# One core, linear attention followed by a gated long convolution: PSUM as four tiles of two banks, gates, forward outputs and inverse products in pairs, the identity matrix made on VectorE, and a new order of the instructions

## The chip, the core and the metric

The kernel runs on one core of one Trainium2 chip. The metric is the device time of one execution in microseconds (us). TensorE (PE) multiplies matrices into PSUM, VectorE (DVE) and ScalarE (ACT) read PSUM and compute elementwise, GpSimd (POOL) makes index patterns and issues the loads, and SyncE (SP) issues the stores and the moves inside the chip's memory.

## The reference, cut to what matters

Eight batches of eight heads, 576 rows of 64 features. An attention with positive random features is followed by a projection to three streams, a circular convolution of the second stream along the rows (in the frequency domain), a product of the three and an output projection.

```python
q_p, k_p = phi(q * scale), phi(k * scale)        # exp(x @ omega.T - |x|^2/2 - max) / sqrt(128)
kv = einsum('bhsm,bhsd->bhmd', k_p, v);  z = sum(k_p, axis=2)
attn = einsum('bhsm,bhmd->bhsd', q_p, kv) / (einsum('bhsm,bhm->bhs', q_p, z)[..., None] + 1e-6)
x = attn.transpose(0, 2, 1, 3).reshape(8, 576, 512)
x1, x2, x3 = split(x @ w_proj, 3)
y = x1 * irfft(rfft(x2, axis=1) * rfft(filter_fft, axis=0), n=576, axis=1) * x3
out = y @ w_out                                   # (8, 576, 512) float32
```

## The kernel before, in words

The 576 rows of a batch are four tiles of 128 rows and a rest of 64; the rests of two batches share one tile ("left", "rest"). The batches are worked in four pairs.

The attention of a batch has these stages, named in the code by `nc.at(...)`. "keys" turns the loaded keys (`transposes`, L634, eight 128x128 transposes into one PSUM tile, copied to `kt` or `klt` by VectorE), multiplies them with omega and takes the exponential on ScalarE into `ek` (`key_features`, L678). "values" finds the largest feature of each row (`max_to_c`, tiles `h1` and `mx`) and scales the values with its reciprocal (`vc`, `vcl`). "queries" gives `eqt` in the same way. "sums" multiplies `ek` with `vc` into `kv`. "turn out" multiplies `eqt` with `kv`, divides (`normalise`, L698: `rden`, then `xb`) and turns the result into `xt` (`turn_runs`, `turn_back`). For batches 5 to 7 the turns of keys, queries and output are DMA transposes issued by SP (`cross`).

The second half has the stages "fold" and "rest" (sums of thirds of the rows, `xf`, times the middle third of `wproj` into `x2`), "gates" (L1054: for each of four column blocks a product `p1` and a product `p3`, each four matmuls of 512 columns; ScalarE copies `p1` to `x1`, VectorE multiplies `p3` with it into `x13`), "forward" (L1152: four products with the tables `fwb`, `fwa`, copied by ScalarE one by one to `sp` and `xs`; SP swaps the halves of `sp` into `sw`), a product with the filter's spectrum (`hps`, `hqs`, made once from the loaded filter and moved by SP), "inverse" (L1215: for each of two column blocks a pair of products in `pa` and then two products `pb`, each added to `ya` by VectorE, two subtractions and two products into `yt` and `ytl`) and "out" (products with `wout`, scaled by ScalarE, stored by SP).

PSUM has eight banks of 512 fp32 values. Before, they are held by three rings (L269 to L276): two tiles of two banks ("a2": features, queries, sums, turn out), three of one bank ("h": everything of the second half) and one of one bank ("t": transposes).

Nothing of this is issued as it is called. A `Plan` records each operation (consecutive matmuls into one tile form one operation) and works out which one depends on which; then `issue` sends them out in the order of the constant `ORDER`, a list of all 1,349 operation numbers written out by hand. An operation of the list goes to the end of its engine's queue, and each engine takes its queue strictly in order; so the list sets the order on PE, ACT, DVE, POOL and SP, the order of the loads among them, and which tile of a ring is taken when. All matmul, copy and load lines of the profile carry the line of that call, L228, so groups are told apart by their tiles.

At the start, `first_constants` (L323) makes the index patterns `fi` and `si` with iota on POOL and the 128x128 identity with the library's `make_identity`, also on POOL; every transpose needs the identity. `make_residues` and `sines` (from L403 and L472) work out the sine tables from `si`, on ACT (`yt`, then the sines) and DVE in turns.

```python
def two_banks():
    return nc.tile(psum, [P, 2, 512], FP32, name="a2", bufs=2)
def bank():
    return nc.tile(psum, [P, 512], FP32, name="h", bufs=3)
def bank_t():
    return nc.tile(psum, [P, 512], FP32, name="t", bufs=1)
...
for op in self.order():
    for real, name, args, kw in op.calls:
        ...
        getattr(real, name)(*args, **kw)
```

Of the kernel before, what the change touches and what calls it, by code (L numbers as in the profile page):

```python
# [12 lines left out]
FP32 = mybir.dt.float32  # L13
# [8 lines left out]
P = 128  # L22
# [4 lines left out]
31 32 28 30 4 3 29 35 26 37 38 55 0 1 2 39 22 5 44 40 45 41 42 139 48 7 46 141 36 11 49 27 70 47 10  # L27
50 43 69 33 51 52 8 34 6 71 57 23 25 53 54 140 72 73 58 24 74 84 85 137 75 586 587 15 60 62 63 86 59
87 64 56 211 585 61 96 66 88 68 590 97 21 65 89 90 91 12 210 67 9 148 106 108 92 17 149 151 153 150
152 154 100 593 101 102 155 107 103 94 109 157 159 98 156 158 588 104 99 105 142 110 112 164 111 113  # L30
13 160 161 114 162 165 136 163 146 20 19 82 79 76 16 145 115 122 123 124 119 222 223 125 126 180 120
127 181 121 116 117 234 235 170 118 14 166 167 93 591 168 95 169 172 628 134 135 175 171 177 128 129
225 173 595 216 629 623 227 130 131 18 592 594 597 624 178 179 174 228 589 229 236 77 81 630 176 194
237 144 132 143 133 195 196 644 599 596 632 224 219 214 226 248 600 188 615 631 189 190 249 617 191
185 80 147 607 192 193 609 230 232 186 187 605 238 598 201 202 78 606 218 182 220 633 231 239 240
197 198 601 183 203 204 603 602 294 625 295 184 616 205 604 618 645 199 206 200 669 207 646 656 657
650 666 608 611 233 613 246 722 612 247 610 241 208 347 724 256 209 257 659 346 250 258 288 259 667
660 670 671 672 636 665 627 260 296 298 251 252 673 282 674 658 661 262 723 614 289 138 253 254 291
668 243 290 649 648 662 293 292 647 687 675 634 358 725 255 688 297 299 261 626 359 242 244 689 637
638 641 635 640 690 264 370 639 642 676 681 304 682 305 263 265 371 663 707 709 710 364 221 306 664  # L40
708 269 277 212 217 480 213 683 307 684 308 685 309 686 654 643 651 655 278 270 279 365 215 701 702
711 266 320 321 677 703 271 267 268 678 652 322 704 360 653 272 691 695 245 692 680 696 679 698 323
324 731 318 273 706 362 302 303 319 730 732 619 712 699 694 697 700 621 274 275 693 733 300 341 718
749 342 343 276 620 301 750 751 720 372 310 312 752 373 622 753 754 738 743 755 714 280 740 739 315
311 756 713 757 719 744 281 317 313 351 83 741 721 705 726 734 374 742 745 746 747 758 810 314 367
728 811 736 316 483 352 344 345 369 735 785 786 787 325 812 326 715 284 285 286 283 349 473 829 830
327 788 817 789 737 748 790 818 328 329 330 828 375 727 813 814 729 376 716 377 717 759 361 366 782
368 363 386 387 388 389 287 479 783 836 336 382 333 334 335 424 837 383 760 815 816 885 844 761 762
350 348 418 845 331 332 887 791 337 765 338 792 793 339 340 763 764 766 820 832 431 430 881 432 433
883 357 384 886 882 378 380 833 767 819 884 427 426 834 822 385 429 428 821 390 888 784 768 770 391  # L50
769 852 835 823 853 485 392 831 434 435 397 399 826 356 450 827 394 771 396 773 379 772 850 776 851
451 400 354 401 436 437 438 398 824 777 838 439 825 839 393 395 452 774 775 864 865 778 779 840 841
454 846 475 847 453 848 410 411 913 872 915 866 867 873 405 780 412 381 353 854 406 407 781 448 449
843 842 849 855 800 468 469 889 413 801 870 871 802 470 471 869 414 858 856 862 794 472 797 415 795
484 355 798 891 416 868 488 491 417 861 914 857 859 425 490 860 879 916 893 922 895 402 863 493 476
806 796 799 420 917 807 919 918 874 403 404 408 809 441 445 409 447 443 878 880 808 923 894 920 896
921 477 421 419 875 1008 906 905 907 890 897 924 925 927 908 899 892 926 877 876 440 444 446 803 804
442 928 898 900 989 929 930 933 492 487 931 489 932 934 992 455 456 457 1007 939 993 994 901 940 461
462 463 941 494 1015 903 942 464 478 990 458 995 482 474 943 1072 1016 1074 1073 902 465 805 459 466
1031 460 1075 904 935 422 486 936 938 909 495 937 496 467 1029 911 1030 1032 1064 1066 950 513 497  # L60
955 952 951 956 953 944 945 1065 1067 498 515 514 518 516 499 500 501 1009 502 954 536 957 503 910
958 507 946 960 1084 520 538 539 1086 540 964 965 541 1085 912 1023 1087 562 1011 991 542 543 563
545 970 971 1024 1060 1062 544 1061 1076 1078 999 508 1012 1010 959 998 505 1063 481 1000 967 1013
1014 947 948 509 510 511 968 517 519 564 1005 1001 996 969 972 1002 966 982 423 512 546 565 1006 997
566 983 521 1025 1045 1003 522 523 1033 1046 949 547 548 549 526 527 528 550 551 524 1017 537 1026
979 1027 1028 525 1004 980 1018 1019 984 532 533 1034 1020 961 962 985 986 534 529 1035 530 1077
1069 1043 531 1022 1021 1044 504 506 560 1040 1041 1079 1042 1037 963 981 988 535 1038 973 556 1036
561 974 1068 1070 580 1080 558 1039 1107 553 581 1071 1082 582 1187 1108 1110 1111 1109 555 1092
1096 1094 1099 552 987 1047 975 1048 1058 557 1168 1101 1098 1097 1100 1102 1103 1057 559 1051 583
1112 1113 1104 1093 554 1095 573 574 1106 1081 570 1173 1083 1052 1049 1050 1174 1088 1090 584 1105  # L70
575 1089 571 567 1114 1115 1116 1140 1141 572 1053 1059 1091 976 576 577 1054 1247 1142 1143 977
1144 1249 1145 568 1055 1186 1056 1188 578 1243 1245 1171 1172 1118 1119 1120 1248 569 1121 1123
1250 1117 1122 1124 1244 1125 579 1246 1126 1169 1128 1190 1191 1149 1150 1129 1194 1131 1195 1178
1170 1189 1259 1130 1261 1239 1241 1132 1134 1196 1135 1133 1177 1136 1137 1139 1179 1210 1192 1211
1197 1193 1175 1176 1202 1203 1260 1204 1151 1208 1262 1205 1184 1138 1182 1209 1185 1198 1199 1127
1152 1183 1153 978 1201 1200 1206 1207 1240 1161 1242 1220 1219 1212 1213 1221 1214 1180 1271 1181
1162 1163 1230 1273 1154 1164 1231 1165 1166 1167 1272 1216 1274 1217 1218 1228 1229 1224 1225 1222
1223 1232 1155 1156 1227 1215 1157 1226 1275 1276 1277 1263 1265 1233 1235 1278 1280 1264 1279 1281
1266 1234 1282 1158 1159 1251 1253 1286 1283 1284 1252 1288 1287 1254 1291 1292 1289 1255 1146 1290
# [57 lines left out]
class Plan:  # L137
# [14 lines left out]

    def at(self, stage, b):
        self.where = stage, b

    def _new(self, eng, name):
        op = Op(eng, len(self.ops), name, self.where)
        self.ops.append(op)
# [1196 lines left out]
```

## Time and profile before

| what | value |
|---|---|
| three runs | 261.46, 261.57 and 497.8 us; median 261.57 us |
| the profiled execution | 261.35 us, of which the span from its first to its last instruction is 259.6 us |
| granted TensorE clock | 0.999 |
| PE busy / ACT busy / DVE busy / POOL busy in the span | 238.8 / 195.6 / 210.6 / 63.4 us |
| PE busy from 0 to 32.5 us, from 32.5 to 227.5, from 227.5 to 259.6 | 18.7 of 32.5, 192.1 of 195.0, 28.0 of 32.1 us |
| exponentials and copies of 128x1024 from PSUM on ACT | 1.03 to 1.04 us each |
| copies of 128x512 from PSUM on ACT | 0.59 to 0.60 us each |
| bytes moved | 35.26 MB, mean 136 GB/s |

The profile is of one execution. A row of a timeline reads: start in us from the span's start, duration in us, engine, line, operation, out<-in by the program's names, shape, and in brackets the engine's idle time before it and what ended it. Operations of one engine overlap somewhat: of two in a row the second starts before the first has ended. In the page's slices each digit is the busy share of a fortieth of the span in tenths.

### The profile page before, as it was taken

The page shows a single profiled execution, that of the slowest core. Times are in us where ns is not written, and L with a number is a line of the kernel's source. Part 1 is how long each engine was busy: PE and PEld are TensorE (multiplying, and loading weights), DVE is VectorE, ACT ScalarE, POOL GpSimd, SP SyncE. Part 2 cuts the span into 40 slices and gives each one's busy share as a digit, 9 for nine tenths or more (in the row PEclk, how much of TensorE's full clock was granted, in tenths as well). Part 3 has the DMA queues.
Part 4 walks back from the last instruction along what each step waited for, and adds up shares of the span by engine and source line. Part 5 has one row for each costly group of instructions (what it writes and reads, how often), then busy time and mean ns, then how long its engine had stood idle before and what let it go on. Part 6 is the DMA issues. An engine that isn't in the chain of part 4 may idle for free.

```text
span 259.6 us, 5722 instructions
## 1 busy us (share of the span) xinstructions
PE 238.8 (92%) x2218; PEld 136.5 (53%) x2250; DVE 210.6 (81%) x474; ACT 195.6 (75%) x309; POOL 63.4 (24%) x88
## 2 busy tenths in 40 slices
PE   0488789999999999999999999999999999999994
PEld 0355555655656656555663554546556554465441
DVE  4889998399998899797899685998989974398880
ACT  3999399899898969999697939977584655575543
POOL 8374843870018610533039000000000000000000
PEclk9999999999999999999999999999999999999999
DMA  5999999999239999699979955027660160053226
GB/s 66 165 147 189 193 200 202 176 185 173 44 94 153 170 201 147 91 209 172 169 182 158 186 102 107 3 76 166 188 162 0 43 167 37 24 161 121 108 80 217
DMA packets 86786, 35.26 MB, mean 136 GB/s; under 512 B 58219, under 2 KB 81256, under 8 KB 86760
## 3 DMA queue, kind: packets, MB, share of 16 engines
q0 software_dynamic: 59616, 17.31, 64.1%
q1 hardware_dynamic: 27000, 17.47, 27.4%
q8 instruction: 17, 0.28, 0.4%
q10 hardware_dynamic: 144, 0.13, 0.1%
q14 instruction: 9, 0.07, 0.1%
HBM read 34.64 MB, written 9.44 MB: 170 GB/s over the span
## 4 chain that ended last, share of the span: by engine, by line
PE 82%; DVE 10%; ACT 4%; issue 2%; POOL 1%; DVEq 0%; POOLq 0%; ACTq 0%
PE h L228 64%; PE a L228 13%; PE t L228 5%; DVE h L228 2%; ACT L228 1%; DVE bt L228 1%; DVE xb L228 1%; DVE vc L228 1%; ACT yt L228 1%; DVE kt L228 1%; DVE qt L228 1%; ACT gtab L228 1%; DVE mx L228 0%; DVE x L228 0%; ACT xt L228 0%
## 5 line engine op out<-in xcount | busy, mean ns | idle before, releaser
L228 PE MATMUL h<-xt,wproj 128*128 128x512 bf16 x244 | 62.6, 379 | 0.6
L228 ACT CAST x<-h 128x512 bf16<-128x512 f32 x68 | 39.7, 596 | 12.4 <-PE h L228 11.4
L228 PEld LDWEIGHTS <-wproj 128*128 128x128 bf16 x384 | 31.3, 98 | 25.8 <-issue 1.7
L228 ACT ACTIVATE osb<-h 128x512 f32<-128x512 f32 (+4 forms) x49 | 27.6, 567 | 16.4 <-PE h L228 9.5
L228 ACT ACTIVATE eqt<-a 128x1024 bf16<-128x1024 f32 x32 | 32.6, 1042 | 1.3 <-PE a L228 1.3
L228 ACT ACTIVATE ek<-a 128x1024 bf16<-128x1024 f32 x32 | 32.3, 1031 | 1.0 <-PE a L228 0.7
L228 PE MATMUL h<-wproj,xf 128*128 128x512 bf16 x124 | 31.9, 380 | 0.2
L228 PE MATMUL h<-wout,yt 128*128 128x512 bf16 x122 | 31.3, 379 | 0.6 <-DVE yt L228 0.2
L228 DVE TENSOR_TENSOR x<-h,x 128x512 bf16<-128x512 f32 x32 | 21.8, 686 | 11.6 <-PE h L228 10.9
L228 POOL DMA_DIRECT2D qn<-in_q_dram x26 | 23.2, 901 | 26.6 <-DMA qt<-qn 15.4
L228 DVE TENSOR_TENSOR bt<-h,osb 128x384 f16<-128x384 f32 x32 | 16.9, 551 | 9.6 <-PE h L228 5.4
L228 PEld LDWEIGHTS <-xf 128*128 128x128 bf16 x134 | 12.5, 100 | 13.4 <-issue 1.0
L228 PE MATMUL h<-x,fwb 128*128 128x512 bf16 x65 | 18.6, 379 | 0.4 <-issue 0.2
L228 PEld LDWEIGHTS <-yt 128*128 128x128 bf16 x128 | 11.6, 98 | 13.5 <-DVE yt L228 0.7
L228 DVE TENSOR_TENSOR xb<-a,rden 128x512 bf16<-128x512 f32 x24 | 16.3, 688 | 0.5
L228 PE MATMUL h<-gtab,xs 128*128 128x384 bf16 x64 | 15.7, 327 | 0.1
L228 ACT CAST xs<-h 128x512 bf16<-128x512 f32 x16 | 9.4, 595 | 8.3 <-PE h L228 8.1
L228 PEld LDWEIGHTS <-eqt 128*128 128x128 bf16 x256 | 11.5, 98 | 6.1 <-DVE xb L228 1.2
L228 PE MATMUL a<-om,kt 64*128 64x128 bf16 x256 | 11.9, 226 | 2.2 <-DVE kt L228 1.5
L228 PE MATMUL a<-kv,eqt 128*128 128x65 bf16 x256 | 12.8, 194 | 1.0 <-DVE xb L228 0.7
L228 PE MATMUL t<-ident,kn 128*128 128x128 bf16 x80 | 6.9, 237 | 7.2 <-POOL ident masks.py:199 6.9
L228 PEld LDWEIGHTS <-kt 64*128 64x128 bf16 x256 | 8.2, 97 | 7.9 <-issue 4.2
(157 smaller groups left out, 479.8 us busy)
## 6 DMA issues: line engine op xcount, KB each, us to landing
out_dram<-osb SPq DMA_DIRECT2D x24, 256.0 KB, 2.3
vn<-in_v_dram POOLq DMA_DIRECT2D x8, 512.0 KB, 7.3
kn<-in_k_dram POOLq DMA_DIRECT2D x7, 512.0 KB, 9.7
qn<-in_q_dram POOLq DMA_DIRECT2D x24, 128.0 KB, 8.0
sw<-sp SPq DMA_DIRECT2D x16, 128.0 KB, 2.4
wproj<-in_moe_w_proj_dram POOLq DMA_DIRECT2D x3, 512.0 KB, 12.1
qn<-in_q_dram POOLq DMA_DIRECT2D x2, 512.0 KB, 8.8
out_dram<-xf SPq DMA_DIRECT2D x4, 256.0 KB, 2.0
```

Of the source, the lines that this page charges most:

```text
L228: getattr(real, name)(*args, **kw)
```

## The change

All of PSUM becomes one ring of four tiles of two banks (name "a2"). `bank` and `bank_t` take such a tile and use its first bank alone. The two products of a gate block (`p1`, `p3`), the outputs 2 and 3 and the outputs 0 and 1 of a forward transform, the rest's two products and the two products `pb` of an inverse block share a tile, one bank each; the new `split` keeps their matmuls separate operations in the plan. The forward outputs are now copied two at a time (one ScalarE copy of 128x1024 in place of two of 128x512), and the two additions of an inverse block are one (128x768 in place of two of 128x384). Gates keep their copy and their product.

The identity is no longer made by `make_identity` on POOL, but by one VectorE comparison of the pattern `si` with a new iota `fp` (the partition's number).

The list `ORDER` is new throughout: it has 1,318 operations, and the order on every engine differs. In the head, POOL issues both halves of the first keys ahead of the iotas, the first two parts of `wproj` (the gates') ahead of the values of batch 1, and the filter later; PE has the transposes of both key halves, omega and the left keys first, gates of batch 0 stand ahead of the sums of batch 1, and all four turns of batch 0's output come before them too. On ACT the dummy sine comes first, so that two table loads are issued in place of three. On SP the transposing DMA of the keys of batch 5 stands ahead of the first swaps and of the filter's moves.

```diff
--- before.py
+++ after.py
@@ -24,63 +24,62 @@
 ORDER = """
-31 32 28 30 4 3 29 35 26 37 38 55 0 1 2 39 22 5 44 40 45 41 42 139 48 7 46 141 36 11 49 27 70 47 10
...
+29 30 31 33 34 32 35 139 0 56 27 28 57 8 1 3 4 38 140 39 2 40 6 23 5 41 42 43 45 46 47 50 49 44 51
...
 """
@@ -143,6 +142,7 @@
         self.nc, self.tc = nc, tc
         self.ops = []
         self.where = "start", 0
+        self.fresh = False
         self.tensor = Proxy(self, "PE", nc.tensor)
         self.vector = Proxy(self, "DVE", nc.vector)
         self.scalar = Proxy(self, "ACT", nc.scalar)
@@ -152,6 +152,9 @@
 
     def at(self, stage, b):
         self.where = stage, b
+
+    def split(self):
+        self.fresh = True
 
     def _new(self, eng, name):
         op = Op(eng, len(self.ops), name, self.where)
@@ -177,6 +180,7 @@
         last = self.ops[-1] if self.ops else None
         join = (
             eng == "PE"
+            and not self.fresh
             and last is not None
             and last.eng == "PE"
             and last.where == self.where
@@ -184,6 +188,8 @@
                 last.writes[0][0] == outs[0].tensor.name
             )
         )
+        if eng == "PE":
+            self.fresh = False
         if join:
             op = last
         else:
@@ -267,13 +273,13 @@
     psum = ctx.enter_context(tc.tile_pool(name="psum", bufs=4, space=bass.MemoryType.PSUM))
 
     def two_banks():
-        return nc.tile(psum, [P, 2, 512], FP32, name="a2", bufs=2)
+        return nc.tile(psum, [P, 2, 512], FP32, name="a2", bufs=4)
 
     def bank():
-        return nc.tile(psum, [P, 512], FP32, name="h", bufs=3)
+        return nc.tile(psum, [P, 2, 512], FP32, name="a2", bufs=4)[:, 0]
 
     def bank_t():
-        return nc.tile(psum, [P, 512], FP32, name="t", bufs=1)
+        return nc.tile(psum, [P, 2, 512], FP32, name="a2", bufs=4)[:, 0]
 
 
     nat_tiles = {}
@@ -318,6 +324,7 @@
     nc.sync.dma_start(out=om_f[:], in_=omega[:, :])
     ident = nc.tile(const, [P, P], BF16, name="ident")
     fi = nc.tile(const, [P, 4], FP32, name="fi")
+    fp = nc.tile(const, [P, 1], FP32, name="fp")
     si = nc.tile(hy, [P, 1024], FP32, name="x2", bufs=2)
 
     def first_constants():
@@ -327,7 +334,10 @@
         for r in (slice(0, 64), slice(64, 128)):
             iota(fi[r, 1:3], pattern=[[-385, 2]], base=385, channel_multiplier=3)
         iota(si[:, 0 : 2 * CH], pattern=[[1, 2 * CH]], base=0, channel_multiplier=0)
-        nc.opaque("POOL", lambda: make_identity(tc.nc, ident[:]), ident[:], 650.0)
+        iota(fp[:], pattern=[[0, 1]], base=0, channel_multiplier=1)
+        nc.vector.tensor_scalar(
+            out=ident[:], in0=si[:, 0:P], scalar1=fp[:, 0:1], scalar2=None, op0=ALU.is_equal
+        )
         nc.where = was
 
     load_main(0, "k", 2, first_constants)
@@ -1056,20 +1066,22 @@
             x13 = nc.tile(hy, [P, CB, SM], BF16, name="x13", bufs=3)
             x13s.append(x13)
             for nb in range(CB):
-                p1, p3 = bank(), bank()
+                two = two_banks()
+                p1, p3 = two[:, 0], two[:, 1]
                 for pp, off in ((p1, 0), (p3, 2 * DM)):
+                    nc.split()
                     for ct in range(CB):
                         nc.tensor.matmul(
-                            out=pp[:],
+                            out=pp,
                             lhsT=wproj[:, ct, off + nb * P : off + (nb + 1) * P],
                             rhs=xt_tiles[b][:, ct, 0:SM],
                             start=(ct == 0),
                             stop=(ct == CB - 1),
                         )
                 x1 = nc.tile(hy, [P, DM], BF16, name="x1", bufs=2)
-                nc.scalar.copy(out=x1[:], in_=p1[:])
+                nc.scalar.copy(out=x1[:], in_=p1)
                 nc.vector.tensor_tensor(
-                    out=x13[:, nb, :], in0=p3[:], in1=x1[:], op=ALU.mult
+                    out=x13[:, nb, :], in0=p3, in1=x1[:], op=ALU.mult
                 )
 
         def spectrum(xs, sp, sw):
@@ -1156,28 +1168,29 @@
                 sp = nc.tile(hy, [P, 2, DM], BF16, name="sp", bufs=2)
                 xss.append(xs)
                 sps.append(sp)
-                for m in (2, 3, 0, 1):
-                    pf = bank()
-                    if m < 3:
-                        for kt_ in (2, 0, 1):
+                for pair in ((2, 3), (0, 1)):
+                    two = two_banks()
+                    for m in pair:
+                        pf = two[:, m % 2]
+                        nc.split()
+                        if m < 3:
+                            for kt_ in (2, 0, 1):
+                                nc.tensor.matmul(
+                                    out=pf,
+                                    lhsT=fwb[:, 3 * m + kt_, :],
+                                    rhs=x2[:, kt_, :],
+                                    start=(kt_ == 2),
+                                    stop=(kt_ == 1),
+                                )
+                        else:
                             nc.tensor.matmul(
-                                out=pf[:],
-                                lhsT=fwb[:, 3 * m + kt_, :],
-                                rhs=x2[:, kt_, :],
-                                start=(kt_ == 2),
-                                stop=(kt_ == 1),
+                                out=pf, lhsT=fwar[:, bb, :], rhs=x2l[:], start=True, stop=False
                             )
-                    else:
-                        nc.tensor.matmul(
-                            out=pf[:], lhsT=fwar[:, bb, :], rhs=x2l[:], start=True, stop=False
-                        )
-                        nc.tensor.matmul(
-                            out=pf[:], lhsT=fwa[:], rhs=x2[:, 3, :], start=False, stop=True
-                        )
-                    nc.scalar.copy(
-                        out=xs[:, m, :] if m < 2 else sp[:, m - 2, :], in_=pf[:]
-                    )
-                    if m == 3:
+                            nc.tensor.matmul(
+                                out=pf, lhsT=fwa[:], rhs=x2[:, 3, :], start=False, stop=True
+                            )
+                    nc.scalar.copy(out=(xs if pair[0] == 0 else sp)[:], in_=two[:])
+                    if pair[0] == 2:
                         sw = nc.tile(hy, [P, 2, DM], BF16, name="sw", bufs=2)
                         nc.sync.dma_start(out=sw[lo64], in_=sp[hi64])
                         nc.sync.dma_start(out=sw[hi64], in_=sp[lo64])
@@ -1193,8 +1206,10 @@
             gates(2 * i + 1)
             nc.at("rest", 2 * i + 1)
             x13l = nc.tile(hy, [P, CB, 2, SL], BF16, name="x13l", bufs=1)
-            p1, p3 = bank(), bank()
+            two = two_banks()
+            p1, p3 = two[:, 0], two[:, 1]
             for pp, off in ((p1, 0), (p3, 2 * DM)):
+                nc.split()
                 for nb in range(CB):
                     for ct in range(CB):
                         nc.tensor.matmul(
@@ -1205,9 +1220,9 @@
                             stop=(ct == CB - 1),
                         )
             x1 = nc.tile(hy, [P, DM], BF16, name="x1", bufs=2)
-            nc.scalar.copy(out=x1[:], in_=p1[:])
+            nc.scalar.copy(out=x1[:], in_=p1)
             nc.vector.tensor_tensor(
-                out=x13l[:].rearrange("p n b s -> p (n b s)"), in0=p3[:], in1=x1[:], op=ALU.mult
+                out=x13l[:].rearrange("p n b s -> p (n b s)"), in0=p3, in1=x1[:], op=ALU.mult
             )
 
             ytl = nc.tile(hy, [P, CB, 2, SL], BF16, name="ytl", bufs=1)
@@ -1234,23 +1249,24 @@
                     nc.scalar.copy(out=ya[:, 0], in_=pav)
                     nc.scalar.mul(out=ya[:, 1], in_=pav, mul=3.0)
                     y = nc.tile(hy, [P, 2, 3, CH], FP16, name="bt", bufs=2)
+                    two = two_banks()
                     for u in range(2):
                         ns = slice((2 * g + u) * P, (2 * g + u + 1) * P)
-                        pb = bank()
+                        nc.split()
                         for m in range(3):
                             nc.tensor.matmul(
-                                out=pb[:, 0 : 2 * CH],
+                                out=two[:, u, 0 : 2 * CH],
                                 lhsT=sp[:, 0, ns] if m == 2 else xs[:, m, ns],
                                 rhs=gtab[:, m, :],
                                 start=(m == 0),
                                 stop=(m == 2),
                             )
-                        nc.vector.tensor_tensor(
-                            out=y[:, u, 0:2],
-                            in0=pb[:, 0 : 2 * CH].rearrange("p (j r) -> p j r", j=2),
-                            in1=ya[:, 0, u].unsqueeze(1).to_broadcast([P, 2, CH]),
-                            op=ALU.add,
-                        )
+                    nc.vector.tensor_tensor(
+                        out=y[:, :, 0:2],
+                        in0=two[:, :, 0 : 2 * CH].rearrange("p u (j r) -> p u j r", j=2),
+                        in1=ya[:, 0].unsqueeze(2).to_broadcast([P, 2, 2, CH]),
+                        op=ALU.add,
+                    )
                     nc.vector.tensor_tensor(
                         out=y[:, :, 2], in0=y[:, :, 0], in1=y[:, :, 1], op=ALU.add
                     )
```

## The prediction

> **What bounds the kernel now.** I read the page first, for the sums over the span and its slices.
>
> ```profile
> span 259.6 us, 5722 instructions
> ...
> PE 238.8 (92%) x2218; PEld 136.5 (53%) x2250; DVE 210.6 (81%) x474; ACT 195.6 (75%) x309; POOL 63.4 (24%) x88
> ...
> PE   0488789999999999999999999999999999999994
> ...
> DVE  4889998399998899797899685998989974398880
> ACT  3999399899898969999697939977584655575543
> ...
> DMA  5999999999239999699979955027660160053226
> ```
>
> TensorE is full from the sixth or seventh slice to the last; only the head and the very end have room. Busy time does not say how full, since matmuls overlap, so I count columns. Groups of four 512-column matmuls start 0.86 us apart (236.18 and 237.04 in the timeline): 0.215 us each, 0.42 ns a column. The program issues 556,672 columns: 233.8 us of PE work. The last matmul ends at 255.8 us, so 22.0 us are lost in all. The timeline of PE says where.
>
> ```profile
> 6.94 1.01 PE L228 MATMUL t<-ident,kn 128*128 128x128 bf16 x8 [6.94 <-POOL ident masks.py:199]
> ...
> 10.82 0.59 PE L228 MATMUL t<-ident,kl 128*128 128x128 bf16 x4 [2.62 <-DVE om L228]
> ...
> 30.03 0.43 PE L228 MATMUL a<-kv,eqt 128*128 128x65 bf16 x8 [0.49 <-DVE xb L228]
> ...
> 31.80 0.61 PE L228 MATMUL t<-ident,xb 128*128 128x128 bf16 x4 [0.79 <-DVE xb L228]
> ...
> 36.75 0.19 PE L228 MATMUL a<-vcl,ekl 128*128 128x65 bf16 x1
> 36.78 0.29 PE L228 MATMUL a<-vc,ek 128*128 128x65 bf16 x4
> ...
> 41.13 1.02 PE L228 MATMUL h<-xt,wproj 128*128 128x512 bf16 x4
> ```
>
> The rows at 36.8 end the key sums of batch 1 ("sums 1"). In the program's order 16.4 us of PE work stand up to there, and they end at 37.0: 20.6 of the 22.0 us are lost by then, and 1.4 us in the 219 us after. The first dense filler (gates, h<-xt,wproj) starts at 41.1. So the change can win only in the first 37 us, and can lose anywhere after.
>
> What paces the head is the third reading, the timelines of ACT and DVE.
>
> ```profile
> 12.79 1.02 ACT L228 ACTIVATE ek<-a 128x1024 bf16<-128x1024 f32 x1
> ...
> 26.41 0.59 ACT L228 CAST kv<-a 128x520 bf16<-128x520 f32 x1 [0.59 <-PE a L228]
> 29.58 0.58 ACT L228 COPY qlt<-t 128x512 bf16<-128x512 bf16 x1 [2.57 <-PE t L228]
> 31.11 1.02 ACT L228 ACTIVATE eqt<-a 128x1024 bf16<-128x1024 f32 x1 [0.95 <-PE a L228]
> ```
>
> ACT starts its exponentials at 12.8, after three table loads, does 13 of them in a row, then idles 3.5 us before 31.1 while DVE works off rden, xb and kt. The chain of waits runs through DVE from 17.8 to 35.6. Loads land in the order of issue: by the trace's semaphores v of batch 0 at 20.9, v of batch 1 at 31.4, wproj at 37.5, 41.0 and 46.1. From 16.1 to 33.5 us 2.9 MB (as written) landed: 0.165 MB/us.
>
> **What the Trainium skill says.** "ScalarE: Activation LUTs", What ACT_TABLE_LOAD costs: about 1283 ns; the trace agrees (1283 ns, three). "Perfetto Trace Analysis", Optimizing Scalar/DVE Operations: a fixed cost per operation, about 51 ns for ScalarE and 125 ns for VectorE on PSUM, so pairing is worth little; the trace agrees in size (below). The same page, Optimization Strategy: a gap that repeats on the engine that should be full can mean too few buffers; no such gap shows in this trace after 37 us. "PSUM — Partial Sum Buffer", The four PSUM rules: a matmul's output is at most one bank, so every single-bank user of the new two-bank tiles leaves a bank empty; the six tiles of before become four.
>
> **The change part by part.**
>
> *Pairs.* Forward outputs: 16 ACT copies of 1024 in place of 32 of 512. Two 512 copies in a row take 1.07 and one 0.60, so one more costs 0.48; two exponentials of 1024 take 1.95 and one 1.03, so 0.92. Gain 16 x 0.04 = 0.6 us of ACT. Inverse: 16 adds of 768 for 32 of 384; 384 takes 0.551 and 512 0.687, 1.06 ns a column, so 768 about 0.96 against 1.02 for two: 1.0 us of DVE. Both are hidden under PE (ACT 75% and DVE 81% busy); if the cover failed in the tail they would be worth under 0.1 us there. Gates keep their copies and products: nothing.
>
> *Identity.* It needs si (iota on POOL), now behind both halves of the first key load (0.92 + 0.76 us from 0.84) and the other iotas (0.32, 0.15, a new one, 0.47): ready about 3.75, in place of 2.86. ACT's first yt then starts at 3.8 (before 4.27, because the first table load waited) and ends at 4.45. In DVE's order the identity stands behind nine residue operations that wait for the yt; before, they took from 5.00 to 9.22. After: 4.5 + 3.7 = 8.2 us for the identity, against 6.9. All of PE waits behind it, and on DVE two small residue fixes, the copy kt and om. So the start is lost by 1.3 us (bounds 0 and 2).
>
> *The first exponential.* With four tiles, the transposes of both key halves, omega and the left keys run in a row: 8.2 + 1.0 + 0.3 + 0.5 + 0.9 = 10.9 (before, one t tile: the second half only at 12.17). om is there at 10.6. Key features 11.0, exponential at 11.55 against 12.79. ACT is free by then: one table load fewer (1.28 us), since the first one now serves Sin and the yt. Gain 1.2 us.
>
> *Head, walked to sums 1.* ACT: 13 exponentials at 0.92 to 0.97 with one gap of 0.6 for batch 1's first kt copy. v of batch 0 lands at 21.4 (k of batch 2 now goes ahead of it, but two left loads don't), plus 1.2 for vc: sums 0 at 22.7, kv at 24.1 (26.4 before). q of batch 1 lands at 24.4; turning out batch 0 needs four rden and xb (0.2 + 0.6 each in a row) from 25.7 to 28.9, then four turns, and ACT's four xt copies end at 32.0, where before the last one, put behind sums 1, ended at 40.35. The moved loads: wproj's two gate parts go ahead of v of batch 1; from 15.1 us (1.625 MB) at 0.165 to 0.17, they land at 27.9 and 31.0, and v of batch 1 at 34.0 (31.4 before). vc ends at 35.6. In the meantime PE has filler that it lacked: four gate groups, 16 x 0.215 = 3.4 us, from 32.5. Sums 1 starts at 36.7 (tile free after batch 0's gate product) and ends at 38.0. By then the new order has issued 21.6 us of PE work. Lost: 38.0 - 21.6 = 16.4, against 20.6. **Gain 4.2 us.** Bounds: 6 (loads quicker), 1 (below).
>
> *After the head.* SP: the cross transpose of keys 5 now stands ahead of the swaps xw and sw and the filter's hps and hqs; it waits for k of batch 5 (about 59 us by bytes) and takes 6.6, and the first user of what is queued behind it comes after 65 us of PE work, 82 us: hidden. w_proj's third part lands at 41 and is wanted at 42 to 43. PSUM: from 40 to 100 us of PE work, a tile's banks are taken again a median of 1.71 us after their last write (2.56 before); from 160 on 2.13 (1.49 before). The readers need 1.03 (exponential) or 0.2 + 0.69 (rden, xb). Summing ACT's and DVE's queues up to each reader against the PE work issued meanwhile, I find no group after sums 1 that comes short by more than a few tenths in either order. Nearest row of before: 1.4 us lost after 37. I add 0.4 (bounds -0.5 and +18, below).
>
> *Tail.* Before, PE waits 0.17 us for yt at 252.19 and in gaps of about 0.1. The new order keeps five groups (4.3 us) between the last inverse product and the last output, and DVE's chain there is 3.5 us plus gate product and yt, 1.4: about even, -0.2.
>
> Sum: -4.2 + 0.4 - 0.2 = -4.0 on the profiled execution's 261.35 (span 259.6): 257.3; it stands 0.2 under the median 261.57, so 257.5.
>
> **The rivals.**
>
> *Loads set the head* (0.20). For: DMA reads 9 from the second slice on, and v of batch 1 is later by 2.6 us. Against: it has no gap now either. At 0.15 MB/us v lands at 36.7, sums 1 ends at 40.5, gain 1.7: 260. The late identity passed on in full ends about there too.
>
> *Loads and ACT quicker than walked* (0.14): v of batch 1 at 32.2, sums 1 at 36.2: gain 6, 255.5.
>
> *Slower: four tiles are too few* (0.16). Place: 40 to 160 us of PE work, 167 tiles. With 1.71 us to reuse, an exponential (1.03 + 0.05) leaves 0.63: one 512 copy ahead of it on ACT fits (0.48), two (0.96) come 0.33 late. A third of the tiles so: 56 x 0.33 = 18.5 us, 276. It decides (past 266.8, beyond 2%) from 28 tiles. Against: the queue sums above.
>
> **How the numbers follow.** The forecast (256 to 259.2) has 0.50, so 257.5. About 2%, 5.2 us, is what a measurement of this kernel can tell from no change. Faster: 0.14 and a third of the forecast's 0.50, 0.30. Slower: 0.14 of the third rival. The rest is 0.56. Range 254.5 to 265.5: it leaves out the third rival's far end and little below.
>
> **What would show it.** Right: PE starts near 8.2 behind DVE's ident; the first exponential near 11.5; two table loads; gates before sums 1; sums 1 ends near 38; PE dense afterwards. Wrong: PE waits for ACT or DVE of a few tenths repeated after 45 us (third rival), vc waiting for the v load past 36 (first), or a last matmul not 3.5 to 4.5 us earlier than 255.8.

## The result and the profile after

| | before | after |
|---|---|---|
| median (executions) | 261.6 us (261.5 to 263.1) | 274.0 us (271.0 to 274.6) |
| profiled execution (its span) | 261.35 (259.6) us | 271.0 (269.2) us |
| PE's last matmul ends at | 255.8 us | 264.7 us |
| mean granted clock of the profiled execution | 0.999 | 0.990 |

The changed kernel is slower: the ratio of the mean times is 1.043, 95% interval 1.034 to 1.052, where 0.984 was forecast. Measured again beside the experiments, it is 273.7 us against 261.6, ratio 1.043 (1.039 to 1.048). Single executions in a slow state, such as the one of 497.8 us before, are left out of every median and ratio.

The page of the kernel after, its busy times and slices (PEclk is the granted TensorE clock, in tenths of full speed):

```profile
span 269.2 us, 5682 instructions
...
PE 239.6 (89%) x2218; PEld 139.3 (52%) x2250; DVE 210.2 (78%) x459; ACT 193.8 (72%) x292; POOL 62.6 (23%) x87
...
PE   0687969999978898999999999989997999999993
...
PEclk9997999999999999999999999999999999999998
```

PE is as busy as before (239.6 and 238.8 us), over 9.6 us more span. Before, its slices were full from the seventh on; now there are sevens and eights between the twelfth slice and the thirty-first. The forecast's own marks in the head come true: in the timeline of PE the transposes start behind VectorE's identity at 8.87 (8.2 was forecast), and gates stand ahead of the sums of batch 1. But one row should not be there:

```profile
8.87 1.01 PE L234 MATMUL a<-ident,kn 128*128 128x128 bf16 x8 [8.87 <-DVE ident L234]
...
32.98 1.02 PE L234 MATMUL a<-xt,wproj 128*128 128x512 bf16 x3
36.23 1.02 PE L234 MATMUL a<-xt,wproj 128*128 128x512 bf16 x4 [2.23 <-ACT x L234]
...
40.80 0.29 PE L234 MATMUL a<-vc,ek 128*128 128x65 bf16 x4
```

The row at 32.98 is p1 of a gate block (the record of one of its four matmuls is missing), the one at 36.23 its p3. Between them PE stands 2.2 us until ACT's copy of p1, `x` in the trace, has ended. p3 doesn't use that copy. The same pair in the middle, PE's rows first and then those of ACT's timeline:

```profile
74.33 1.03 PE L234 MATMUL a<-xt,wproj 128*128 128x512 bf16 x4
77.00 1.02 PE L234 MATMUL a<-xt,wproj 128*128 128x512 bf16 x4 [1.64 <-ACT x L234]
```

```profile
74.53 1.01 ACT L234 CAST sp<-a 128x1024 bf16<-128x1024 f32 x1
75.44 1.02 ACT L234 COPY qt<-a 128x1024 bf16<-128x1024 bf16 x1
76.34 0.61 ACT L234 CAST x<-a 128x512 bf16<-128x512 f32 x1
```

p1 is done at 75.4, but ACT has `sp` and `qt` to do first, starts the copy of p1 at 76.34 and ends it at 76.95; p3 starts 0.05 us later. PE's waits, the longest in total first:

```profile
PE a L234 <- ACT x L234: 10.0, 11, 2.2
PE a L234 <- DVE ident L234: 8.9, 1, 8.9
PE a L234 <- ACT eqt L234: 1.3, 3, 0.5
PE a L234 <- DVE qt L234: 1.1, 1, 1.1
```

Eleven waits for ACT x, 10.0 us, of 0.3 to 2.2 us each, all in front of gate products (one of them a rest's). The group of the gates' matmuls, before and after, with its idle time at the end of the line:

```profile
L228 PE MATMUL h<-xt,wproj 128*128 128x512 bf16 x244 | 62.6, 379 | 0.6
L234 PE MATMUL a<-xt,wproj 128*128 128x512 bf16 x245 | 62.0, 379 | 10.6 <-ACT x L234 9.7
```

The program that is built from the kernel agrees: the first matmul of p3 waits for a semaphore of ScalarE in 21 of the 22 blocks whose copy of p1 stands ahead of p3 in the list.

### The profile page after: what moved, and what is told of

The parts are those of the page before. It is cut to its first block, busy times and chain, and to the rows that moved or that the text cites. A ratio compares the mean times of both kernels' runs of the same rounds, so it can differ in the third digit from the quotient of the medians.

```text
span 269.2 us, 5682 instructions
## 1 busy us (share of the span) xinstructions
PE 239.6 (89%) x2218; PEld 139.3 (52%) x2250; DVE 210.2 (78%) x459; ACT 193.8 (72%) x292; POOL 62.6 (23%) x87
## 4 chain that ended last, share of the span: by engine, by line
PE 73%; ACT 14%; DVE 5%; DMA 3%; issue 3%; POOL 0%; ACTq 0%; DVEq 0%
PE a L234 73%; ACT x L234 4%; DMA vn<-in_v_dram 3%; ACT ek L234 2%; ACT eqt L234 2%; ACT xt L234 1%; ACT osb L234 1%; DVE xt L234 1%; DVE x L234 1%; ACT qt L234 1%; ACT eql L234 1%; DVE vc L234 0%; ACT xtl L234 0%; DVE yt L234 0%; ACT xs L234 0%
## 5 line engine op out<-in xcount | busy, mean ns | idle before, releaser
L234 PE MATMUL a<-xt,wproj 128*128 128x512 bf16 x245 | 62.0, 379 | 10.6 <-ACT x L234 9.7
L234 ACT CAST x<-a 128x512 bf16<-128x512 f32 x68 | 39.8, 594 | 33.5 <-PE a L234 33.2
L234 DVE TENSOR_TENSOR x<-a,x 128x512 bf16<-128x512 f32 x32 | 22.0, 690 | 21.8 <-PE a L234 12.0
L234 ACT ACTIVATE osb<-a 128x512 f32<-128x512 f32 (+4 forms) x49 | 27.6, 571 | 13.0 <-PE a L234 10.4
L234 POOL DMA_DIRECT2D qn<-in_q_dram x26 | 23.3, 901 | 38.8 <-PE a L234 15.3
L234 PE MATMUL a<-wproj,xf 128*128 128x512 bf16 x121 | 31.6, 380 | 0.7 <-DVE xb L234 0.2
L234 PE MATMUL a<-wout,yt 128*128 128x512 bf16 x122 | 30.9, 379 | 0.3
L234 DVE TENSOR_TENSOR bt<-a,osb 128x768 f16<-128x768 f32 x16 | 15.2, 952 | 5.7 <-ACT osb L234 5.6
L234 PEld LDWEIGHTS <-xf 128*128 128x128 bf16 x134 | 12.1, 99 | 12.8 <-DVE xf L234 0.5
L234 PE MATMUL a<-x,fwb 128*128 128x512 bf16 x70 | 18.3, 380 | 0.2
L234 PE MATMUL a<-gtab,xs 128*128 128x384 bf16 x64 | 15.6, 326 | 0.0
L234 PE MATMUL a<-om,kt 64*128 64x128 bf16 x256 | 12.3, 229 | 0.7 <-ACT eqt L234 0.5
L234 POOL DMA_DIRECT2D kn<-in_k_dram x9 | 8.0, 889 | 20.7 <-DMA kt<-kn 12.8
L234 PE MATMUL a<-vc,ek 128*128 128x65 bf16 x256 | 11.9, 199 | 0.6 <-DVE vc L234 0.6
```

## The experiments

Theory A: p1 and p3 now share a PSUM tile. They lie in different banks, and the plan (which compares regions) sees no tie between the copy of p1 and p3; but the program that is built from it makes p3, a write into the tile, wait for the copy, a read of the tile. Theory B, the prediction's slow rival: four tiles of two banks are too few. Times are medians; the kernel before had 261.55 us in the first set, 261.6 to 261.75 in the others. A "tie" below is such a wait between instructions that share nothing but a tile.

**The changed kernel again.** 

> The changed kernel unaltered, as the yardstick of this set. Both theories: 271 to 275 us, with about eleven waits of TensorE for ScalarE's copies x, 10 us in all. If the lower granted clock (0.99 where the kernel before had 0.999) comes from the waits, it shows here again; if it was that chip's, it does not.

273.7 us, clock 0.978 to 0.998. The trace names ten waits for ACT x, 7.8 us; the eleventh, 2.2 us ahead of the same first p3 (here at 37.23, when ACT's copy has just ended at 37.17), it puts down to a load, `kl`. So the eleven waits repeat, and so does the lower clock.

**Copies put behind p3, or ahead of it.** In the list, shown for two blocks (620 and 1049 are p1, 621 and 1050 p3, 622 and 1051 the copy):

```diff
-620 228 622 621
+620 228 621 622
```

> The changed kernel with one edit in the order: in the 22 gate blocks where ScalarE's copy of p1 stands ahead of the product p3 in the list, the copy is put directly behind p3. TensorE's own order stays. Theory A (p3 shares its tile with p1, so that p3 is made to wait until the copy of p1 has read the tile, though it lies in the other bank): the 10.0 us of waits for ACT x go, some of them come back as waits for the next reader; 261 to 264 us, TensorE waits for ACT x below 1 us, granted clock 0.99 or more. Theory B (four tiles are too few, a tile is wanted before its reader is done): the waits move to the next tile, 268 us or more.

```diff
-1049 1050 492 494 1051
+1049 1051 1050 492 494
```

> The opposite of the run before: in the 14 gate blocks where the copy of p1 stood behind p3, it is put between p1 and p3, so that all 36 have this order. Theory A: each of the 14 now makes TensorE wait for the copy, at least 0.6 us for the copy and 0.1 for the hand-over, more where ScalarE has other work first: 14 x 0.75 = 10 us or more, 281 us or above. Theory B: the tiles are taken and freed in the same order, 0 to 2 us.

Behind p3: 268.2 us, 5.5 less. Ahead of p3 in all 36: 282.0, 8.3 more, with 20 waits for ACT x, 15.3 us. The second is A's number and excludes B's. The first is B's number (268 or more), not A's. PE's waits in it say why:

```profile
PE a L234 <- DVE x L234: 2.9, 7, 0.7
...
PE a L234 <- DVE x13l L234: 1.6, 2, 1.4
...
PE a L234 <- ACT x L234: 0.7, 1, 0.7
```

Waits for ACT x are down to 0.7 us, but 4.5 us have come for DVE's products of p3 with the copy, the last readers of gate tiles. That is either B, or A turned round: a copy behind p3 has to wait until p3 has been written, 0.86 us, though it reads only p1, and the tile is held that much longer. The changed kernel itself shows this second direction, in a block whose copy stands behind p3. PE's row holds p1 and p3, eight matmuls:

```profile
37.50 1.90 PE L234 MATMUL a<-xt,wproj 128*128 128x512 bf16 x8
```

```profile
39.44 0.59 ACT L234 CAST x<-a 128x512 bf16<-128x512 f32 x1 [0.80 <-PE a L234]
```

p1 is written after half of PE's row, at about 38.5; but ACT stands idle for 0.80 us and starts the copy at 39.44, 0.04 us after p3's end at 39.40.

**Identity early.** In the list with the copies behind p3 (operation 7 is the comparison that makes the identity; it stood further behind):

```diff
-41 42 43
+41 7 42 43
```

> As the run with the copies behind p3, and the identity's comparison moved in VectorE's order from behind the nine residue operations to ahead of the first of them. Theory A on the head: the identity is there at about 4.5 us in place of 8.8, TensorE starts when the first keys land (5.7), the copy kt follows the residues at about 9.2 in place of 9.9, and the first exponential starts at 11.5 in place of 12.1, held by ScalarE's table load: 0.6 us faster than without it. Rival: the head is paced by the loads of v, so nothing is gained (0 +- 0.2).

266.9 us, 1.3 less than without, but the intervals overlap (1.016 to 1.023 against 1.020 to 1.027): no gain is shown, and neither of the two numbers is excluded.

**Fewer large tiles.** Three kernels with the changed kernel's list and early identity. Where the list would start a tile that is not free, the operation moves back.

```diff
-name="a2", bufs=4
+name="a2", bufs=3                       # second and third kernel: bufs=2
-two = two_banks(); p1, p3 = two[:, 0], two[:, 1]
+p1, p3 = gate_bank()[:], gate_bank()[:] # ring "h" of one-bank tiles: 2, or 4
```

> The changed kernel with its list (copies of p1 where it has them, identity early), and the gates' p1 and p3 taken from a ring of two one-bank tiles of their own, so that only three tiles of two banks are left for all the rest; 69 of the 1,318 operations move back where a tile would not be free. Theory A (the shared tile is what costs: p3 waits for the copy of p1, and with the copy put behind p3 the copy waits for p3, so that the tile is held longer): waits for ACT x fall below 2 us though the rest has a tile less; 259 to 264 us. Theory B (four tiles of two banks are too few): with three it is worse than with four, 270 us or more.

> As the run with the gates in tiles of their own, but PSUM as two tiles of two banks for those who fill two, and four of one bank for all who fill one (turns, folds, gates, outputs): six tiles, as the kernel before had; 35 operations move back. Pairs of forward copies and of additions stay. Theory A: no shared gate tile and no bank left empty, the head's gain of 3.5 us stays: 257 to 260 us, faster than the kernel before. Theory B' (the new list itself is worse in the middle, whatever PSUM is): 264 us or more.

> As the run with two tiles of two banks and four of one, and the forward outputs copied one by one and the inverse products added one by one again, from one-bank tiles. Both theories: 0.6 us more on ScalarE and 1.0 us more on VectorE, hidden under TensorE: within 1 us of the run with pairs. Rival: pairs hold a two-bank tile that features need; undone, it is 1 us or more faster.

288.2, 287.0 and 288.0 us. All miss A's numbers and look like B. They don't decide, though. 69 operations of the list had to move in the first and 35 in the second, so each is a new list as well as a new ring; and in the first some 17 us of PE's waits go to ACT x, osb, eqt, ek and DVE xb alike. They show that a list is tied to its ring; how much of the loss is the missing tiles and how much the moved operations, no run tells. That the pairs make no difference (third against second: 1 us, with overlapping intervals) fits the prediction's term.

**The tie cut, everything else kept.** 

```diff
-nc.scalar.copy(out=x1[:], in_=p1)
+nc.scalar.copy(out=x1[:], in_=xt_tiles[b][:, 0, 0:SM])
```

> The changed kernel with its list untouched, in which ScalarE's copy x1 reads the gate's input (xt, for the rest xtl) in place of the product p1. That leaves the product with p1 out of the output; each engine has the same number of instructions of the same size, the tiles, their number and the list are the same, but p3 has no reader of its tile to wait for, nor the copy p3. Theory A (the shared gate tile, both ways, is what costs): the waits for ACT x and those for DVE x nearly go, the head's 3 us stay: 257 to 260 us, granted clock 0.995 or more. Theory B (four tiles of two banks are too few for this list): 266 us or more, the waits move to other readers.

> The kernel before with ScalarE's copy x1 reading xt (xtl for the rest) in place of p1, so without the product with p1: the control for the same edit in the changed kernel. Theory: here p1 and p3 have tiles of their own and the copy is no wait of TensorE's, so nothing changes, within 1 us of 261.6. Rival (the edit itself saves time, by the copy no longer waiting for p1): 3 us or more faster.

260.8 us in the changed kernel, 12.8 less and 0.8 beyond A's range, ratio to before 0.996 (0.993 to 0.998); 261.7 in the kernel before, ratio 1.000 (0.998 to 1.001). So the edit itself saves nothing where the tiles are separate, and with the same list and the same four tiles the whole loss goes. The clock did not come as A expected: 0.983 to 1.000, not 0.995 or more. PE's waits that are left, as the trace lists them:

```profile
PE a L234 <- DVE ident L234: 8.9, 1, 8.9
PE a L234 <- ACT eqt L234: 1.3, 3, 0.5
PE a L234 <- DVE qt L234: 1.1, 1, 1.1
PE a L234 <- DMA kt<-kn: 1.1, 1, 1.1
PE a L234 <- DVE mk L234: 1.0, 1, 1.0
PE a L234 <- ACT ek L234: 0.3, 2, 0.2
```

No wait for a gate's reader is left, neither ACT x nor DVE x. B falls: four tiles are enough for this list. A stands, in both directions; a kernel that computes everything has yet to show the same.

**Versions that compute everything.** With the early identity: the copy behind p3 only where a wait had shown or could hide; p1 and p3 in two tiles of the ring in all blocks; and in two tiles only where the copy stands ahead of p3.

```diff
-two = two_banks()
-p1, p3 = two[:, 0], two[:, 1]
+if (b, nb) in ONE_TILE:                 # 13 blocks, and the rest of pair 7
+    two = two_banks()
+    p1, p3 = two[:, 0], two[:, 1]
+else:
+    p1, p3 = bank(), bank()             # the second version: always
```

> The changed kernel, identity early, and the copy of p1 put behind p3 only in the 15 gate blocks where the profile of the changed kernel showed, or may hide, a wait before p3; in seven it stays ahead. Theory A: in those seven the copy is done sooner and the tile freed sooner than with all 22 behind: 1 to 3 us faster than the run with all copies behind p3 and identity early (266.9), 264 to 266. Theory B: the same, 266.9 +- 0.5.

> The changed kernel with identity early, its four tiles and its list (three operations move), but p1 and p3 in two tiles of the ring, each using one bank of its tile. No copy waits for p3 and no p3 for a copy; a gate block takes two of the four tiles. Theory A: what is shared costs more than the tile more: waits for ACT x before p3 go, waits for a tile come, 262 to 266 us. Theory B (tiles are short): 270 us or more.

> The changed kernel with its list and its four tiles, identity early; p1 and p3 share a tile only in the 14 gate blocks whose copy stands behind p3 in the list, and take two tiles, one bank of each, in the 22 blocks whose copy stands ahead of p3. Nothing else moves. Theory A (only a p3 that has to wait for the copy, and a copy that has to wait for p3 where the list did not mean it to, cost): no wait for ACT x before p3 beyond 1 us in all, the tiles are held about as long as the list meant; 258.5 to 261 us, faster than the kernel before and near the run whose copy reads xt. Rival (blocks that take two tiles shorten the ring for all others): 263 to 265, as with two tiles in all blocks.

265.7, 264.1 and 261.4 us. The first two lie in A's ranges and outside B's. The third keeps the four tiles of the changed kernel and, but for the early identity, its list, and is 12 us faster than it: 0.998 of the kernel before (0.996 to 1.000), 0.4 us beyond the slow edge of what was expected. Of PE's waits, the longest that is not for a load, and the one for readers of gate tiles:

```profile
PE a L237 <- ACT eqt L237: 1.6, 4, 0.5
...
PE a L237 <- DVE x L237: 0.4, 2, 0.2
```

No wait for ACT x is listed. Where p3 stands ahead of the copy anyway, sharing costs next to nothing.

**The clock in the head.** The changed kernel has a lower granted clock in some stretches of the head, and not the same ones in each execution. The windows 20 to 24, 24 to 28 and 36 to 40 us of the repeated changed kernel, then the first two of the version of 261.4 us (after the stretch and its length the busy times of PE, PEld, DVE, ACT and POOL, then PEclk, the mean granted clock, the DMA share and GB/s):

```profile
20.00:24.00 4.00, 1.78 (x28) 1.28 (x26) 3.19 (x7) 4.00 (x5) 0.88 (x1) 0.96 1.61 190
24.00:28.00 4.00, 4.00 (x74) 3.56 (x72) 2.74 (x7) 1.62 (x3) 2.25 (x3) 0.61 1.43 200
36.00:40.00 4.00, 2.77 (x8) 0.77 (x8) 2.74 (x6) 1.60 (x3) 2.53 (x3) 0.67 1.69 186
```

```profile
20.00:24.00 4.00, 1.77 (x36) 1.47 (x36) 3.24 (x6) 4.00 (x5) 0.88 (x1) 1.00 1.60 189
24.00:28.00 4.00, 3.68 (x84) 3.04 (x80) 3.86 (x12) 2.58 (x4) 2.25 (x3) 1.00 1.39 201
```

PE is as idle from 20 to 24 us in both, but the clock falls only in the first. What a fall costs can be read there. Two matmul groups of the repeated changed kernel, p3 of the first gate block and the block behind it, took 1.02 and 1.90 us in the profile with a clock of 1.00 at that place (the rows at 36.23 and 37.50 above); at 0.67 they took:

```profile
37.23 1.77 PE L234 MATMUL a<-xt,wproj 128*128 128x512 bf16 x4 [2.22 <-DMA kl<-in_k_dram]
...
39.47 2.53 PE L234 MATMUL a<-xt,wproj 128*128 128x512 bf16 x8
```

The two profiles differ by 2.6 us of span: the gates start 1.0 us later (33.98 against 32.98) behind the slow stretch from 24 us on, and sums 1 ends 2.6 us later (43.5 against 40.9) behind the second slow stretch. The edit puts nine more matmuls into PE's waits for qt and vc:

```diff
+for _ in range(5):                      # queries of batch 0; four more in its sums
+    nc.tensor.matmul(out=ps[:, 0, :], lhsT=ident[:],
+        rhs=ekl[:, 0:4].rearrange("p m c -> p (m c)"), start=True, stop=True)
```

> The changed kernel unaltered but for nine more matmuls of 512 columns, whose results are overwritten: five at the head of batch 0's first query product, four at the head of its sums, where TensorE waited 1.1 us for qt and 0.6 to 1.2 us for vc. Theory (the granted clock falls where TensorE has idled in the head, and the fall after 24 us costs about 1 us): the clock stays at 1.00 from 20 to 30 us, mean 0.99 or more in most runs, median 1 to 2 us below 273.7. Rival: the lower clock has another cause (shared tile waits later, or the chip), no change of time or 1 us more for the added work.

> The same nine matmuls in the kernel whose gates share a tile only where it is free. Theory: its runs fall into two groups, 260.4 us at a clock of 0.996 or more and 262 at 0.985 to 0.991; with the fill nearly all fall into the first: median 260.4, 1 us faster than without. Rival: no change, or up to 1 us slower by the added 1.9 us of work.

The clock follows: 0.991 to 1.000 in the changed kernel, 0.995 to 1.000 in the last version. The median doesn't: 273.3 against 273.7, 261.2 against 261.4. The single executions say why. Unfilled, the last version has two groups, 11 executions of 260.3 to 261.1 us at a clock of 0.996 to 0.999 and 11 of 261.7 to 262.4 at 0.984 to 0.991; filled, its 21 have 261.2 in the middle, 0.7 slower than the first group's 260.5 and 0.7 faster than the second's 262.0. In the repeated changed kernel the one execution at 0.998 took 270.8 us and those at 0.978 to 0.983 273.6 to 274.1; filled, one at 1.000 took 272.1. So an execution with the falls takes about 1.5 us longer in the one kernel and about 3 in the other, and as far as these executions show, the fill costs about what it saves.

**Parts of the head.**

```diff
-19 14 17 20      # w2, vl, w0, v of batch 1
+14 20 19 17
```

> The kernel whose gates share a tile only where it is free, with the loads of v and vl of batch 1 issued ahead of the two first parts of wproj, as the kernel before had it. The prediction's step: wproj's parts are at 31 and 34 us in place of 27.9 and 31.8, v at 28.4 in place of 34.0; the list has the gates of batch 0 ahead of the sums of batch 1, so TensorE waits for wproj to 34.2 in place of 33.2: about 1 us slower, 262.4. Rival (the loads of v set the head): sums 1 come earlier, 1 us or more faster.

> The kernel before with one part of the change: the identity made by VectorE's comparison, ahead of VectorE's residue operations, the new iota directly behind the pattern's. Theory: the identity is there at about 3.8 us in place of 6.9, in VectorE's idle time from 2.9 to 5.0; TensorE starts at 5.6 when the first keys have landed, but the copy kt and om stay behind the residues (9.5), and ScalarE's third table load holds the first exponential: 0.2 to 0.7 us faster, 261. Rival: TensorE's first start is not what paces the head: 0 +- 0.2.

> The kernel before with the early identity of the earlier run, and the dummy sine put first on ScalarE (its zero ahead on VectorE), so that two table loads are issued in place of three: the head's second part of the change, alone. Theory (the first exponential waits for ScalarE's table loads; the identity alone left it at 12.8): the sines start 0.9 us earlier, the first exponential at about 11.9, and the chain behind it passes on 0.5 to 0.9 us: 260.8 to 261.2. Rival (the head is paced further on, by the loads of v and VectorE's turn out): 261.7 +- 0.3.

Loads in the old order: 261.5 us, about 0.2 more, intervals overlapping, so neither of the two expectations came true. wproj's parts land at 30.2 and 32.7, sooner than expected, and the gates start at 33.46 in place of 32.48: of this one microsecond next to nothing reaches the end. The identity alone in the kernel before: 261.9, ratio 1.000 (0.999 to 1.002), though PE starts at 5.74 in place of 6.94: the rival was right. With the third table load gone as well: 261.0, ratio 0.996 (0.994 to 0.998), the lowest median of the kernels that compute everything, though not clear of the filled last version's. ACT's timeline, the identity alone and then with two loads:

```profile
11.52 1.28 ACT L228 ACT_TABLE_LOAD   x1
12.81 1.02 ACT L228 ACTIVATE ek<-a 128x1024 bf16<-128x1024 f32 x1
```

```profile
9.63 1.28 ACT L228 ACT_TABLE_LOAD   x1
10.92 1.02 ACT L228 ACTIVATE ek<-a 128x1024 bf16<-128x1024 f32 x1
```

The exponential follows the load at once in both. It is 1.9 us earlier, and 0.7 of these reach the end.

## Why the prediction was wrong

The sum was -4.2 (head) + 0.4 (after it) - 0.2 (tail) = -4.0. Measured by the same count (time at a point, less the PE work issued by then):

| term | forecast | after | tie cut (copy of xt) | last version (one tile only where free) |
|---|---|---|---|---|
| to the end of sums 1 (21.6 us of work) | -4.2 | 40.9 - 21.6 = 19.3, against 20.6 before: -1.3 | 40.2 - 21.6 = 18.6: -2.0 | 38.7 - 21.6 = 17.1: -3.5 |
| from there to PE's last matmul | +0.4 | 264.7 - 233.8 - 19.3 = 11.6, against 1.4: +10.2 | 254.5 - 233.8 - 18.6 = 2.1: +0.7 | 254.8 - 233.8 - 17.1 = 3.9: +2.5 |
| behind the last matmul | -0.2 | 4.5 against 3.8: +0.7 | 4.6: +0.8 | 4.5: +0.7 |
| sum (of spans) | -4.0 | +9.6 | -0.5 | -0.3 |

These are profiled executions, at clocks of 0.990 (after), 0.983 (tie cut) and 0.997 (last version). The one of the changed kernel is its fastest of the first set, 3.0 us under the median of 274.0; by the section on the clock, most of these 3 us are the lower clock of the other executions.

**The step that failed** is a clause of the pairs' paragraph: "Gates keep their copies and products: nothing." The copies and products are the same, but p1 and p3 went from two tiles to one, and that added a wait that no dependency of the plan holds. It put a wait of 2.2 us into the head and, with 7.8 us of idle time in ten waits, 9.5 of the 10.2 us after it: with the tie cut 0.7 are left. (A wait costs some 0.17 us more than the profile's idle time, as the matmul before it is modelled to end that much later than the next could start: at 77.00, 1.64 idle and 1.81 lost.) The queues "up to each reader" had been worked out from the plan's dependencies, which don't hold this wait; the built program's do, and 21 of them stand on p3.

**The slow rival had the right size by a wrong mechanism, that is by luck.** "Four tiles are too few" gave 276 us from a third of 167 tiles 0.33 us late. Measured were 274, but from eleven waits of 0.3 to 2.2 us, all at gates, and with the tie cut no wait of that kind is left. Its sign, waits of PE for ACT after 45 us, came true for the other cause. The queue sums that spoke against it hold for all but the tie: with it cut, the term after the head is +0.7 where +0.4 was forecast, and one wait of 1.06 us for a DMA transpose of keys (at 149 us) is most of what is lost there.

**Banks and tiles.** The Trainium skill, "Perfetto Trace Analysis", Matmuls, advises to rotate independent matmul groups through different PSUM banks, so that the reading of one by ScalarE or VectorE overlaps with the next. Here different banks were not enough: what counted was the tile, 10.0 us of waits. The wait is put in by the build, not asked for by the hardware: "PSUM — Partial Sum Buffer", PSUM bank collisions raise a hardware error, says that two engines on different banks run clean, and the trace agrees: in the kernel before ACT reads gate products from 43.27 to 44.46, in tiles and banks of their own, while PE writes other banks without a gap.

**The head** was walked nearly right. v of batch 1 landed at 34.0, as forecast, wproj's first two parts at 27.9 and 31.8 (27.9 and 31.0). The identity was 0.7 us late, the first exponential 12.1 (11.55), kv 25.5 (24.1; its 40 matmuls ran at a lower clock), the last xt copy ended at 32.9 (32.0). With separate tiles where it hurt, and the identity early, the gain is 3.5 of 4.2. Its parts were priced less well: moved loads and early identity show no gain by themselves, the saved table load (with the identity early) 0.7 us at the end. The rest is left for the order that puts gates into PE's gaps; no run has that order alone.

**Pairs** hid, as forecast. **Middle:** the last version's +2.5 is more than the +0.7 of the kernel with the tie cut. Seven waits of 0.15 to 0.32 us are listed after 43 us, 1.5 us in all; that they come from the tiles which its blocks take twice is likely and not shown. **The tail** is 0.7 to 0.8 us longer in all three, where 0.2 less was forecast. Of this 0.5 us is that ACT's last output copy starts 0.54 us after PE's last matmul (265.26 against 264.72), where before it started 0.03 us after (255.85 against 255.82): ACT's half of the output that it splits with DVE now waits for DVE's half (0.77 us ahead of 264.40), and before came first. The rest of the tail stays open.

## What to carry to other kernels

When two products are put into one PSUM tile, a reader of one can become a wait for a later write of the other, even in another bank (here in 21 of 22 blocks), and a write that stands ahead delays the reader. Putting both products ahead of the first reader gave back 5.5 of the 12.8 us; tiles of their own where a reader stands between, with an early identity, gave back 12.3. Look for waits in the built program, not in one's own table of dependencies: a planner that compares regions believes in an overlap that the build does not grant. To tell a false tie from too small a ring, redirect the reader to another source of the same size and keep everything else, and make the same edit in the kernel before as a control. Changing the ring itself changes the list's fit: three such kernels took 287 to 288 us and decided nothing.

## What was not expected of the hardware

After a stretch in which PE was busy 1.78 of 4 us, the granted clock fell to 0.61 for the next 4 us, and to 0.67 where PE had stood 2.2 us at a gate. But another kernel's profile has 1.77 busy of 4 us and a clock of 1.00, and the changed kernel's first profile has the same stand of 2.2 us and a clock of 1.00 behind it. The Trainium skill, "TensorE: Matmul & The Clock Gate", HAM oscillation, describes falls behind idle gaps of more than about 3.4 us; here the longest single wait near a fall was 2.2 us, and falls came in some executions and not in others of the same kernel. Filling two waits of about 1 us with matmuls nobody needs lifted the mean clock of an execution from 0.984 to 0.999 up to 0.995 to 1.000 in the last version, and moved its median by 0.2 us, within the noise.
